# State updates as column tiles and carried state times q as row tiles in batches 1 to 3 of a fused retention and mixer kernel

## The chip, the cores and the metric

One core of a Trainium2 chip runs the whole kernel. The metric is the device time of one execution in microseconds (us). Runs of one kernel scatter by 1 to 2 us to either side here, so every timed comparison below is the kernel against the kernel before, executed in turn on the same chip. A profile is one execution of each kernel; its "span" runs from the first to the last instruction and is about 2 us shorter than the device time. A run more than 1.5% above the fastest of its kernel is called slow, the others fast; ratios use fast runs alone.

## The reference

Two stages in sequence. Retention with one decay per head (4 batches, 8 heads, 768 steps, head size 64), then a mixer with a low-rank product over the sequence and an MLP.

```python
state = gamma * state + einsum('bhd,bhe->bhde', k[:, :, t], v[:, :, t])
y[:, :, t] = scale * einsum('bhd,bhde->bhe', q[:, :, t], state)
...                                     # x: y as (batch, 768, 512)
h = xt @ U @ V                          # rank 32, over the sequence
u = x + h.transpose(0, 2, 1)
out = u + maximum(u @ w_ch1, 0) @ w_ch2 # 512 -> 2048 -> 512
```

The kernel runs the recurrence in chunks of 128 steps. Per chunk: scores (k transposed times q, masked), the output (scores times v, plus carried state times q), and the state update (k transposed times v, summed in PSUM over the chunks). Decays are folded into q and k beforehand.

## The kernel before

Batches 1 to 3 run chunk by chunk between pieces of the MLP of the batch in front of them; a list of start points ("at" and "lag") says where between those pieces each block stands. The parts that the change and the argument touch (cuts marked with `...`):

```python
RINGS = {...}        # PSUM banks by use: "s" has two banks, "o" one, "st" one

def turn_dma(b, ci):                     # batches 2 and 3
    ...
    (nc.sync if b > 2 else nc.scalar).dma_start_transpose(
        out=qkT, in_=qkd.rearrange("p n h d -> p (n h d)"))

def state(b, ci):                        # two heads a matmul, 128x128
    ...
    for p in range(4):
        nc.tensor.matmul(st_p[:, ts(p, P)], qkd[:, 1, ds(2 * p, 2)],
                         vb[:, ds(2 * p, 2)], start=(ci == 0 and p == 0), ...)
    for i in range(2):                   # only the diagonal 64x64 squares
        r = ds(D * i, D)
        evac("A", ns[r, :, r], four(st_p)[r, :, r])

def score(b, ci):
    sp = [bank("s") for _ in range(2)]
    for h in range(H):                   # row tiles: even heads 0-63, odd 64-127
        r = ds(D * (h % 2), D)
        nc.tensor.matmul(sp[h % 2][:, ts(h // 2, P)], qkT[r, 4 + h // 2],
                         qkT[r, h // 2], start=True, stop=True)
    ...                                  # VectorE masks into a[0], a[1]

def mix(b, ci):
    o_p = bank("o")
    if ci:
        for p in range(4):               # carried state times q, whole array
            nc.tensor.matmul(o_p[:, ts(p, P)], qkT[:, p], state[:, p], ...)
    for i in range(2):
        for h in range(i, H, 2):
            nc.tensor.matmul(o_p[:, ts(h, D)], a[i][:, h // 2], vb[:, h], ...)
    evac("A", xs[b][:, ci], o_p)         # one ScalarE copy, 128x512
...
lag = [0.12, 0.17, 0.23] if b == 2 else [0.1, 0.12, 0.2]  # state, score, mix
```

The state sits in SBUF as pairs of heads in 128x128 squares whose off-diagonal halves are zero, so half of each whole-array matmul multiplies zeros or is thrown away.

Of the kernel before, what the change touches and what calls it, by code (L numbers as in the profile page):

```python
# [18 lines left out]
def kernel(  # L19
# [11 lines left out]
    nc = tc.nc  # L31
    P = 128
    B, H, S, D = q.shape
# [11 lines left out]
    NST = 4  # L45
# [26 lines left out]
    def bank(tag, dtype=fp32):  # L72
        n_bank[0] += 1
        ring = RINGS[tag]
        ring.append(ring.pop(0))
        return psum.tile([P, 2048 // (4 if dtype == fp32 else 2)], dtype,
                         tag=f"bank{ring[-1]}", name=f"{tag}_{n_bank[0]}",
                         bufs=1)

    def four(t):  # L80
        return t.rearrange("p (n m) -> p n m", n=4)

    def evac(eng, dst, src):
        if eng == "A":
            nc.scalar.activation(dst, src, AF.Copy)  # L85
        else:
            nc.vector.tensor_copy(out=dst, in_=src)  # L87
# [136 lines left out]
    states = []  # L224
    for i in range(NST):
        t = consts.tile([P, 4, P], bf16, name=f"state{i}")
# [68 lines left out]
    xs = {}  # L295
    live = {}
    n_state = [0]
# [20 lines left out]
    def state_half(sc, x):  # L318

        kd, vb = pre["k", sc], pre["v", sc]  # L320
        first = sc == 0 and x == 0
        if first:
            live["st_p"] = bank("st")
            live["st", 0, 0] = None
        st_p = live["st_p"]
        r = ds(HP * x, HP)
        for par in range(2):
            for p in range(4):
                nc.tensor.matmul(st_p[:, ts(p, P)], kd[r, par, ds(2 * p, 2)],  # L329
                                 vb[r, par, ds(2 * p, 2)],  # L330
                                 start=(first and par == 0 and p == 0),
                                 stop=True, skip_group_check=True)
        ns = states[n_state[0] % NST]
        n_state[0] += 1
        for i in range(2):
            ri = ds(D * i, D)
            evac("A", ns[ri, :, ri], four(st_p)[ri, :, ri])
        live["st", sc + x, 1 - x] = ns

    def score_block(sc, par, tag="s", engs="DD"):  # L340
        kT, qT = live["k", sc], live["q", sc]
        sp = [bank(tag) for _ in range(2)]
        for p in range(4):
            for i in range(2):
                for x in range(2):
                    r = ds(D * i, D)
                    nc.tensor.matmul(sp[i][ds(HP * x, HP), ts(p, P)],
                                     kT[r, p, x, ds(HP * par, HP)],
                                     qT[r, p, x], start=True, stop=True,
                                     skip_group_check=True)  # L350
        for i in range(2):
            a = blk.tile([P, 4, P], bf16, tag=f"a0{i}{par}",
                          name=f"a0{i}{par}_{sc}")
            m = mask0[:, par, None, :].to_broadcast([P, 4, P])
            if engs[i] == "D":
                nc.vector.tensor_tensor(a, four(sp[i]), m, op=ALU.mult)
            else:
                t = blk.tile([P, 4, P], bf16, tag="a_raw", bufs=1,
                              name=f"a_raw_{sc}")
                evac("A", t, four(sp[i]))  # L360
                nc.gpsimd.tensor_tensor(a, t, m, op=ALU.mult)
            live["a", sc, par, i] = a
# [45 lines left out]
    def state(b, ci):  # L408
        qkd, vb = pre.pop((b, ci))
        live[b, ci].append(live.get(("state", b)))  # L410
        if ci < NCK - 1:
            if ci == 0:
                live["st_p", b] = bank("st")
            st_p = live["st_p", b]
            for p in range(4):
                nc.tensor.matmul(st_p[:, ts(p, P)], qkd[:, 1, ds(2 * p, 2)],  # L416
                                 vb[:, ds(2 * p, 2)],
                                 start=(ci == 0 and p == 0), stop=True,
                                 skip_group_check=True)
            ns = states[n_state[0] % NST]  # L420
            n_state[0] += 1
            for i in range(2):
                r = ds(D * i, D)
                evac("A", ns[r, :, r], four(st_p)[r, :, r])
            live["state", b] = ns

    def score(b, ci):
# [12 lines left out]
    def mix(b, ci):  # L440
        if ci == 0:
            xs[b] = xp.tile([P, NCK, DM], fp16, tag="x", name=f"x_{b}")
        vb, qkT, state, *a = live.pop((b, ci))
        o_p = bank("o")
        if ci:
            for p in range(4):
                nc.tensor.matmul(o_p[:, ts(p, P)], qkT[:, p], state[:, p],  # L447
                                 start=(p == 0), stop=False,
                                 skip_group_check=True)
        for i in range(2):  # L450
            for h in range(i, H, 2):
                nc.tensor.matmul(o_p[:, ts(h, D)], a[i][:, h // 2], vb[:, h],  # L452
                                 start=(ci == 0 and h == 0), stop=True,
                                 skip_group_check=True)
        evac("A", xs[b][:, ci], o_p)



# [336 lines left out]
    for b in range(1, B + 1):  # L795
# [9 lines left out]
        if b < B:  # L805
# [11 lines left out]
            else:  # L817
# [4 lines left out]
                if b == 2:  # L822
                    for i, f in enumerate(w2_sums(4) + w2_sums(6)):
                        d = 0.04 + 0.025 * i
                        tracks.append(([f], d, d))
                turn = turn_dma
            for i in range(NCK):
                for f, d in ((turn, 0), (state, lag[0]), (score, lag[1]),
                             (mix, lag[2])):
                    tracks.append(([part(f, b, i)], at[i] + d, at[i] + d))  # L830
            t = at[-1] + lag[2]
# [43 lines left out]
```

## Time and profile before

| | before |
|---|---|
| device time, median of 3 runs | 224.11 us (223.7 to 224.51) |
| span of the profile | 223.0 us |
| TensorE busy | 214.5 us, 96% |
| state blocks, carried blocks | 15 and 15, of four 128x128 matmuls each |
| TensorE instructions on the page, matmuls plus weight loads | 2149 + 2152 = 4301 |

TensorE (PE) is the bound; what matters of it is quoted in the prediction (columns: start, length, engine, source line, operation, result and operands, tile, shape, count). Three more places of the same profile also belong here. The first is PE at the first score block of batch 3 (columns: start, length, engine, source line, operation, result and operands, tile, shape, count):

```profile
139.16 0.39 PE L416 MATMUL st<-vd,qkd 128*128 128x128 bf16 x4
139.38 1.03 PE L640 MATMUL mlp<-uT,w1b 128*128 128x512 f16 x4
140.34 0.40 PE L432 MATMUL s<-qkT 64*128 64x128 bf16 x8
```

The score block starts at 140.34 us without a recorded wait, but its operand, a transpose by DMA, landed at 140.29: there is hardly any slack, 0.05 us. The second is the queue that issues these transposes, SyncE's:

```profile
135.61 1.24 SPq L507 DMA_TRANSPOSE uT<-x  x1
136.90 6.91 SPq L404 DMA_TRANSPOSE qkT<-qkd  x5
```

They are issued back to back, 1.2 to 1.3 us each; the first of q and k is issued at 136.90 and lands 3.39 us later. The third is a line of the page that I passed over before predicting, under the DMA queues (packets, MB, share of 16 engines):

```profile
q8 instruction: 17, 0.28, 0.6%
```

Seventeen transfers of 16 KB on a queue of their own fetch instructions. 4301 instructions on 17 fetches is about 253 each.

### The profile page before, as it was taken

The page shows a single profiled execution, that of the slowest core. Times are in us where ns is not written, and L with a number is a line of the kernel's source. Part 1 is how long each engine was busy: PE and PEld are TensorE (multiplying, and loading weights), DVE is VectorE, ACT ScalarE, POOL GpSimd, SP SyncE. Part 2 cuts the span into 40 slices and gives each one's busy share as a digit, 9 for nine tenths or more (in the row PEclk, how much of TensorE's full clock was granted, in tenths as well). Part 3 has the DMA queues.
Part 4 walks back from the last instruction along what each step waited for, and adds up shares of the span by engine and source line. Part 5 has one row for each costly group of instructions (what it writes and reads, how often), then busy time and mean ns, then how long its engine had stood idle before and what let it go on. Part 6 is the DMA issues. An engine that isn't in the chain of part 4 may idle for free.

```text
span 223.0 us, 5337 instructions
## 1 busy us (share of the span) xinstructions
PE 214.5 (96%) x2149; PEld 144.2 (65%) x2152; DVE 142.2 (64%) x284; ACT 88.0 (39%) x180; POOL 83.5 (37%) x121
## 2 busy tenths in 40 slices
PE   7899899999999998999999999999999999999993
PEld 2466644485555553666688874766887856668882
DVE  6478465333947476599996843786868443867452
ACT  3255645465465315657611005767420035550000
POOL 6442578868867775613757602000000000000000
PEclk9999999999999999999999999999999999999999
DMA  5998799999999999999999999920002734000123
GB/s 163 298 291 205 212 342 299 301 388 239 226 206 212 209 251 209 227 299 167 239 203 222 238 206 215 189 45 11 3 0 85 182 116 47 0 0 4 38 105 142
DMA packets 94633, 39.22 MB, mean 176 GB/s; under 512 B 78096, under 2 KB 87312, under 8 KB 94608
## 3 DMA queue, kind: packets, MB, share of 16 engines
q1 hardware_dynamic: 87408, 35.73, 67.8%
q10 hardware_dynamic: 7200, 3.15, 7.2%
q8 instruction: 17, 0.28, 0.6%
q14 instruction: 8, 0.07, 0.1%
HBM read 27.85 MB, written 6.29 MB: 153 GB/s over the span
## 4 chain that ended last, share of the span: by engine, by line
PE 79%; DVE 8%; SPq 5%; DMA 3%; ACT 1%; issue 1%; ACTq 1%; POOL 0%; DVEq 0%; POOLq 0%
PE mlp L640 32%; PE A L562 14%; PE mlp L685 9%; PE C L562 7%; SPq L142 5%; PE B L562 4%; DMA in<-in_q_dram 3%; PE s L432 2%; DVE gS L515 2%; DVE a L437 2%; PE o L452 2%; PE qk L396 1%; PE o L447 1%; PE st L416 1%; PE s L480 1%
## 5 line engine op out<-in xcount | busy, mean ns | idle before, releaser
L640 PE MATMUL mlp<-uT,w1b 128*128 128x512 f16 (+1 forms) x512 | 89.2, 326 | 0.5 <-DVE uT L87 0.5
L647 ACT ACTIVATE gT<-mlp 128x512 f16<-128x512 f32 (+1 forms) x94 | 45.5, 491 | 63.6 <-PE mlp L640 59.3
L640 PEld LDWEIGHTS <-w1b 128*128 128x128 f16 x512 | 48.1, 98 | 30.8 <-issue 1.2
L645 DVE TENSOR_SCALAR gT<-mlp 128x512 f16<-128x512 f32 (+1 forms) x34 | 18.9, 554 | 27.2 <-PE mlp L640 27.2
L437 DVE TENSOR_TENSOR a<-s,mask 128x512 bf16<-128x512 f32 x36 | 23.1, 682 | 10.7 <-PE s L432 10.7
L562 PEld LDWEIGHTS <-gT 128*128 128x128 f16 x288 | 27.4, 98 | 3.8
L264 POOL TENSOR_TENSOR qkd<-in,gk 128x512 bf16<-128x512 f32 x18 | 19.8, 1100 | 13.1 <-DMA in<-in_k_dram 12.6
L264 POOL TENSOR_TENSOR qkd<-in,gq 128x512 bf16<-128x512 f32 x18 | 19.2, 1066 | 13.9 <-DMA in<-in_q_dram 11.4
L685 PE MATMUL mlp<-w2b,gT 128*128 128x512 f16 x96 | 24.2, 380 | 0.0
L562 PEld LDWEIGHTS <-gS 128*128 128x128 f16 x216 | 21.0, 98 | 2.7
L85 ACT ACTIVATE x<-o 128x512 f16<-128x512 f32 x21 | 12.5, 595 | 21.0 <-PE o L452 19.9
L562 PE MATMUL A<-w2t,gT 128*128 128x256 f16 x144 | 18.4, 273 | 0.0
L85 ACT ACTIVATE state<-st 64x256 bf16<-64x256 f32 x40 | 15.0, 375 | 5.0 <-PE st L329 3.8
L262 POOL CAST vd<-in 128x512 bf16<-128x512 f32 x18 | 11.8, 655 | 6.2 <-DMA in<-in_v_dram 3.4
L685 PEld LDWEIGHTS <-gT 128*128 128x128 f16 x96 | 8.1, 98 | 7.2
L178 PE MATMUL mlp<-ones 128*128 128x512 bf16 x32 | 10.3, 451 | 1.8 <-DVE ones L171 1.4
L484 DVE TENSOR_TENSOR x<-s,x 128x256 f16<-128x256 f32 (+1 forms) x16 | 8.2, 552 | 4.6 <-PE st L480 2.4
L291 POOL CAST w2b<-in 128x512 f16<-128x512 f32 x16 | 9.8, 616 | 3.2 <-DMA in<-in_moe_w_ch_dram 2.6
L285 POOL CAST w1b<-in 128x512 f16<-128x512 f32 x16 | 9.6, 615 | 1.8 <-DMA in<-in_moe_w_ch_dram 1.4
L85 ACT ACTIVATE qkT<-qk 128x1024 bf16<-128x1024 bf16 x6 | 6.1, 1024 | 8.3 <-PE qk L396 8.3
L562 PE MATMUL B<-w2b,gT 128*128 128x256 f16 x72 | 9.3, 273 | 0.0
L562 PE MATMUL C<-w2t,gS 128*128 128x256 f16 x72 | 9.3, 273 | 0.0
(116 smaller groups left out, 261.2 us busy)
## 6 DMA issues: line engine op xcount, KB each, us to landing
in<-in_moe_w_ch_dram SPq DMA_DIRECT2D x32, 256.0 KB, 5.8
in<-in_k_dram SPq DMA_DIRECT2D x24, 256.0 KB, 5.4
in<-in_q_dram SPq DMA_DIRECT2D x24, 256.0 KB, 5.4
in<-in_v_dram SPq DMA_DIRECT2D x24, 256.0 KB, 5.6
out_dram<-o SPq DMA_DIRECT2D x12, 256.0 KB, 2.0
out_dram<-o SPq DMA_DIRECT2D x12, 128.0 KB, 4.3
out_dram<-o ACTq DMA_DIRECT2D x6, 256.0 KB, 4.4
Vf<-in_moe_V_dram SPq DMA_DIRECT2D x4, 96.0 KB, 3.8
```

Source lines behind the costliest of these rows:

```text
L85: nc.scalar.activation(dst, src, AF.Copy)
L142: nc.sync.dma_start(out=t, in_=src)
L178: nc.tensor.matmul(idle_bank[0], ones[:, :P], ones, start=True, stop=True, skip_group_check=True)
L262: nc.gpsimd.tensor_copy(out=t, in_=src)
L264: nc.gpsimd.tensor_tensor(t, src, g[:, ci, :, None].to_broadcast([P, H, D]), op=ALU.mult)
L291: nc.gpsimd.tensor_copy(out=w2b[:, m], in_=take("w2", m))
L437: nc.vector.tensor_tensor(a, four(sp[i]), causal(mask), op=ALU.mult)
L562: nc.tensor.matmul(acc[key, i], lhs[:, m, ts(i, P)], rhs[:, m], start=(fresh and m == 0), stop=(m == NH - 1), skip_group_check=True)
L640: nc.tensor.matmul(g_p[:, :sz], w1b[:, c, ts(m, P)], uTs[b][:, ds(j, nj), c], start=(c == 0), stop=(c == NCB - 1))
L645: nc.vector.tensor_relu(gT[:, m, ds(lo, sz)], g_p[:, :sz])
L647: nc.scalar.activation(gT[:, m, ds(lo, sz)], g_p[:, :sz], AF.Relu)
L685: nc.tensor.matmul(ch, gT[:, m, ts(j, P)], w2b[:, m], start=(m == 0), stop=(m == NM - 1))
```

## The change

Terms: a matmul holds one operand in the array as weights and streams the other through it in columns. A row tile uses half of the array's rows (64*128 in the profile lines), a column tile half of its columns (128*64); 128*128 is the whole array. PSUM is the memory that matmuls write to, in banks.

The intent: compute only the 64x64 squares that are needed. The state update of each head becomes a column tile (two heads side by side in the array), carried state times q becomes row tiles that write two banks, and the state is kept compact, so that one copy of 128x256 replaces two of 64x256. The output then needs two banks, and takes the second from the ring "s" of the scores.

```diff
-            for p in range(4):
-                nc.tensor.matmul(st_p[:, ts(p, P)], qkd[:, 1, ds(2 * p, 2)],
-                                 vb[:, ds(2 * p, 2)],
-                                 start=(ci == 0 and p == 0), stop=True,
+            for h in range(H):
+                nc.tensor.matmul(st_p[ds(D * (h % 2), D), ts(h // 2, D)],
+                                 qkd[:, 1, h], vb[:, h],
+                                 start=(ci == 0 and h < 2), stop=True,
...
-            for i in range(2):
-                r = ds(D * i, D)
-                evac("A", ns[r, :, r], four(st_p)[r, :, r])
+            evac("A", ns, heads(st_p))
...
-        o_p = bank("o")
+        o_p = [bank("s"), bank("o")]
         if ci:
-            for p in range(4):
-                nc.tensor.matmul(o_p[:, ts(p, P)], qkT[:, p], state[:, p],
-                                 start=(p == 0), stop=False,
+            for h in range(H):
+                r = ds(D * (h % 2), D)
+                nc.tensor.matmul(o_p[h % 2][:, ts(h // 2, D)], qkT[r, h // 2],
+                                 state[r, h // 2], start=(h < 2), stop=False,
...
-                nc.tensor.matmul(o_p[:, ts(h, D)], a[i][:, h // 2], vb[:, h],
-                                 start=(ci == 0 and h == 0), stop=True,
+                nc.tensor.matmul(o_p[i][:, ts(h // 2, D)], a[i][:, h // 2],
+                                 vb[:, h], start=(ci == 0 and h < 2), stop=True,
...
-        evac("A", xs[b][:, ci], o_p)
+            evac("A", x[:, i], heads(o_p[i]))
```

More of the change, by code (lines that the diff above doesn't have):

```diff
@@ L81, in four, with heads @@
         return t.rearrange("p (n m) -> p n m", n=4)
+    def heads(t):
+        return t[:, :4 * D].rearrange("p (n d) -> p n d", n=4)
     def evac(eng, dst, src):
@@ L414, in state @@
             st_p = live["st_p", b]
-            for p in range(4):
-                nc.tensor.matmul(st_p[:, ts(p, P)], qkd[:, 1, ds(2 * p, 2)],
-                                 vb[:, ds(2 * p, 2)],
-                                 start=(ci == 0 and p == 0), stop=True,
+            for h in range(H):
+                nc.tensor.matmul(st_p[ds(D * (h % 2), D), ts(h // 2, D)],
+                                 qkd[:, 1, h], vb[:, h],
+                                 start=(ci == 0 and h < 2), stop=True,
                                  skip_group_check=True)
-            ns = states[n_state[0] % NST]
+            ns = states[n_state[0] % NST][:, :2].rearrange(
+                "p n (x d) -> p (n x) d", x=2)
             n_state[0] += 1
-            for i in range(2):
-                r = ds(D * i, D)
-                evac("A", ns[r, :, r], four(st_p)[r, :, r])
+            evac("A", ns, heads(st_p))
             live["state", b] = ns
@@ L443, in mix @@
         vb, qkT, state, *a = live.pop((b, ci))
-        o_p = bank("o")
+        o_p = [bank("s"), bank("o")]
         if ci:
-            for p in range(4):
-                nc.tensor.matmul(o_p[:, ts(p, P)], qkT[:, p], state[:, p],
-                                 start=(p == 0), stop=False,
+            for h in range(H):
+                r = ds(D * (h % 2), D)
+                nc.tensor.matmul(o_p[h % 2][:, ts(h // 2, D)], qkT[r, h // 2],
+                                 state[r, h // 2], start=(h < 2), stop=False,
                                  skip_group_check=True)
+        x = xs[b][:, ci].rearrange("p (n two d) -> p two n d", n=4, two=2)
         for i in range(2):
             for h in range(i, H, 2):
-                nc.tensor.matmul(o_p[:, ts(h, D)], a[i][:, h // 2], vb[:, h],
-                                 start=(ci == 0 and h == 0), stop=True,
+                nc.tensor.matmul(o_p[i][:, ts(h // 2, D)], a[i][:, h // 2],
+                                 vb[:, h], start=(ci == 0 and h < 2), stop=True,
                                  skip_group_check=True)
-        evac("A", xs[b][:, ci], o_p)
+            evac("A", x[:, i], heads(o_p[i]))
     us, uTs, pcs = {}, {}, {}
```

## The prediction

> **What bounds the kernel now.** I read the page first: the busy shares and the chain of work that ended last.
>
> ```profile
> PE 214.5 (96%) x2149; PEld 144.2 (65%) x2152; DVE 142.2 (64%) x284; ACT 88.0 (39%) x180; POOL 83.5 (37%) x121
> ...
> PE 79%; DVE 8%; SPq 5%; DMA 3%; ACT 1%; issue 1%; ACTq 1%; POOL 0%; DVEq 0%; POOLq 0%
> ```
>
> TensorE (PE) is busy 96% of the span and carries 79% of the chain; the granted clock is full in every slice. So the change is judged by the PE time that it adds or removes, except where the chain is on another engine. Second, the groups by shape between 52 and 180 us, where batches 1 to 3 run between the MLP pieces of the batch before.
>
> ```profile
> L416 PE MATMUL st<-vd,qkd 128*128 128x128 bf16 x60 | 5.8, 219 | 0.0
> L447 PE MATMUL o<-state,qkT 128*128 128x128 bf16 x60 | 5.8, 219 | 0.0
> ```
>
> These two groups are all that the change touches on PE: 15 blocks of four for the state update, 15 blocks of four for carried state times q. The 219 ns is latency. What a matmul costs is its slot, start to start, and that comes from the timeline. Here is PE around chunk 1 of batch 3:
>
> ```profile
> 142.86 0.39 PE L416 MATMUL st<-vd,qkd 128*128 128x128 bf16 x4
> 143.09 0.60 PE L640 MATMUL mlp<-uT,w1b 128*128 128x256 f16 x4
> 143.52 0.40 PE L452 MATMUL o<-vd,a 128*128 128x64 bf16 x8
> 143.76 0.60 PE L640 MATMUL mlp<-uT,w1b 128*128 128x256 f16 x4
> 144.29 0.40 PE L432 MATMUL s<-qkT 64*128 64x128 bf16 x8
> 144.62 0.61 PE L640 MATMUL mlp<-uT,w1b 128*128 128x256 f16 x4
> ```
>
> A block of four 128x128 matmuls takes 143.09 - 142.86 = 0.22 us, 56 ns each. Four with 256 columns take 0.43 us (143.09 to 143.52), eight with 64 columns 0.24 us (29 ns each). But the four 256-column ones in front of the score block take 143.76 to 144.29 = 0.53 us: PE loses 0.10 us before a block that uses row tiles (64*128). The score block of eight 64x128 then takes 0.33 us. Run two at a time, its four pairs would need 4 x 56 = 0.22 us, so it loses another 0.11 us on the way back to whole-array matmuls. A tiled block pays about 0.21 us for its two changes of tiling. The low-rank projection, in column tiles 128*32, shows the same:
>
> ```profile
> 166.28 1.04 PE L562 MATMUL A<-w2t,gT 128*128 128x256 f16 x8
> 167.25 0.52 PE L470 MATMUL o<-x,Ub 128*32 128x128 f16 x24
> 167.70 0.50 PE L562 MATMUL B<-w2b,gT 128*128 128x256 f16 x3
> ```
>
> Eight of 256 columns need 0.87 us but take 0.97 (0.10 lost going in). The 24 tiles are six groups of four: 6 x 56 = 0.34 us, and they take 0.45 (0.11 lost going out). And this, from batch 0, is the tempo of row-tile pairs with 64 moving columns into two banks:
>
> ```profile
> 15.59 0.19 PE L380 MATMUL o<-v,a 64*128 64x64 bf16 x1
> 15.59 0.19 PE L380 MATMUL qk<-v,a 64*128 64x64 bf16 x1
> 15.62 0.19 PE L380 MATMUL o<-v,a 64*128 64x64 bf16 x1
> 15.62 0.19 PE L380 MATMUL qk<-v,a 64*128 64x64 bf16 x1
> ```
>
> Two start together, the next pair 0.03 us (29 ns) later: tiles of different row groups do run side by side.
>
> **What the Trainium skill says.** "TensorEngine Tiling (Array Packing)", Key Properties, says that changing the tiling mode drains TensorE. It gives no figure; the trace agrees and puts it at about 0.10 us each way. "TensorE: Matmul & The Clock Gate", Part 3 (The mechanism), says that tiles overlap with starts about 4 ns apart; the trace agrees (pairs start together above). The tiling page's Instruction Overhead warns not to take a tiling factor out of a dimension that is already small; here the tiled matmuls move only 64 columns, so a block has little streaming to save. "PSUM — Partial Sum Buffer", PSUM bank collisions, says that different row tiles may not write one PSUM bank at the same time; hence the second bank of this change. No run here shows that error.
>
> **The change part by part.**
>
> (1) State update: 4 matmuls of 128x128 (0.22 us) become 8 of 128x64 in two column tiles. Four pairs at 29 ns are 0.12 us, saving 0.11; entering and leaving the tiling costs 0.21. First-pair fill is in that 0.21. Net +0.11 us a block (0.33 for 0.22).
>
> (2) Carried state times q: the same sum with row tiles, 0.22 to 0.33 us, net +0.11.
>
> (3) 30 such blocks: the instruction order of the changed kernel shows that nothing moves; 29 are surrounded by whole-array work (MLP, transposes, or the 128-row a-times-v). Only chunk 2 of batch 3 has a state block directly before a carried one, which saves one change of tiling. 30 x 0.108 - 0.11 = +3.1 us of PE work.
>
> (4) ScalarE: state evacuation becomes one copy of 128x256 (about 0.385 us, as the 128x256 relu) for two of 64x256 (0.375 each): 15 x 0.365 = -5.5 us. The x evacuation becomes two of about 0.385 for one of 0.594: 18 x 0.18 = +3.2 us. Net -2.3 us on an engine that is 39% busy: worth next to nothing.
>
> (5) Part of (3) falls into waits that PE has anyway. The best case is in batch 2:
>
> ```profile
> 110.07 0.39 PE L447 MATMUL o<-state,qkT 128*128 128x128 bf16 x4
> 110.37 0.29 PE L452 MATMUL o<-vd,a 128*128 128x64 bf16 x4
> 110.97 0.29 PE L452 MATMUL o<-vd,a 128*128 128x64 bf16 x4 [0.31 <-DVE a L437]
> ```
>
> Here the chain of waits lies on VectorE from 99.26 to 110.92 us (gS, gT and masks back to back), and PE waits 0.08 + 0.49 us for the masks, after 0.07 us at 101.5. In that stretch (from 94.3 us on VectorE runs without a gap) PE gets 4 state and 3 carried blocks, +0.76 us, of which 0.63 us vanish. Then 0.05 us at 115.5, 0.10 us at 53.8 (score waits for qkT) and 0.10 of a 0.24 us wait at 76.6. Absorbed together: 0.88 us. Left of (3): +2.2 us.
>
> (6) A new wait. The output now takes a bank of the ring "s", which has two banks, both used by every score block. The next chunk's score block writes its first half to the other bank and its second half to the one that the mix has just used, so its second matmul waits for ScalarE to read the first half of the output. In the changed kernel's instruction order those matmuls do wait for ScalarE. In batches 1 and 2 there is 0.4 to 1.7 us of other matmuls in between, which is enough. In batch 3 three score blocks (148.4, 153.0, 162.0 us) follow the mix at once:
>
> ```profile
> 161.44 0.39 PE L447 MATMUL o<-state,qkT 128*128 128x128 bf16 x4
> 161.66 0.40 PE L452 MATMUL o<-vd,a 128*128 128x64 bf16 x8
> 161.99 0.40 PE L432 MATMUL s<-qkT 64*128 64x128 bf16 x8
> 162.09 0.60 ACT L85 ACTIVATE x<-o 128x512 f16<-128x512 f32 x1 [3.13 <-PE o L452]
> ```
>
> Worked out for this one, counted from the start of the last matmul of the first half: result after 0.193 us (its latency), ScalarE starts about 0.05 later (here 162.09 - 162.06), reads for 0.385, and PE resumes about 0.055 later (qkT to score in batch 1): 0.68 us. PE without a wait gets there after five slots of 29 ns plus 0.10 for the tiling: 0.24 us. Stall 0.44 us. At 153.0 ScalarE is still on a relu (152.67 to 153.27): 0.48. At 148.4 a relu (to 148.45) and the state copy stand in front: 0.60. At 144.3, with 0.43 us of MLP between: about 0.15. Sum +1.7 us.
>
> Sum: 3.1 - 0.9 + 1.7 = +3.9 us, all of it before batch 3 ends. Batch 4's MLP behind it has PE back to back, so it reaches the end.
>
> **The rivals.** (A) The intent: tiles halve the PE time, 30 x 0.11 = -3.2 us, 220.9 us (1.4% faster). For it: the pairs do run side by side, and two ScalarE copies become one. Against: every tiled block in the trace pays 0.2 us. It would need a change of tiling to be free where weights were loaded ahead; the score blocks, loaded ahead too, say no. (B) Only the tiling costs, and the bank is free in time: 226.3 us. For it: the halves are copied separately, so the first starts early. Against: the three score blocks that follow at once. (C) The column tiles run at 56 ns a pair rather than 29, because 64 weight columns can't be loaded fast enough: another 15 x 3 x 27 ns = 1.2 us, 229.2 us. The trace has no 128*64 tile; in batch 0, 64*64 tiles keep 56 ns with 128 moving columns, which doesn't decide it. (D) The extra copies queue behind relus and stall scores in batch 2 as well, where ScalarE also spends 1.46 us issuing a transpose (94.53): +0.5 to 1 us. Against: those copies stand ahead of the next transpose in the queue.
>
> **Range and chances.** 224.1 + 3.9 = 228.0 us. Low end: no stalls, 226.3, rounded to 226.4. High end: C and part of D with the absorption kept, 229.3. Slower by over 2% begins at 228.6, which needs about 0.6 us more than the sum: 0.24. Faster by over 2% needs -4.5 us, more than A gives: 0.02. Within 2%: 0.74.
>
> **What would show it.** In the changed profile: state and carried blocks of eight at 0.33 us including the 0.10 lost in front (right), or 0.12 (A right); pair spacing 29 ns in 128*64 tiles (else C); in batch 3 at three score blocks a PE wait of 0.4 to 0.6 us released by ScalarE's x copy (else B); the gap at 110.4 us shrunk from 0.57 to near nothing; ScalarE's busy time about 2 us down. I am wrong if tiling changes are cheaper beside column tiles, or if VectorE's chain in batch 2 moves with PE, so that nothing is absorbed (then 228.9).

## The result, and the profile after

| | before | after |
|---|---|---|
| device time, median (range), same rounds | 224.31 us (223.7 to 225.12), 4 runs | 230.23 us (229.37 to 231.0), 4 runs |
| ratio, 95% interval | | 1.026, 1.021 to 1.031: slower |
| span of the profile | 223.0 us | 229.2 us |

Ratios here and below are the mean time of one kernel's fast runs over that of the other's fast runs of the same rounds, so not quite the ratio of the medians that are quoted.

The page of the changed kernel, its busy line and its chain of work that ended last:

```profile
PE 219.3 (96%) x2272; PEld 142.1 (62%) x2272; DVE 143.1 (62%) x284; ACT 84.4 (37%) x183; POOL 83.3 (36%) x121
...
PE 75%; DMA 13%; DVE 4%; POOL 2%; ACT 2%; issue 1%; SPq 1%; DVEq 0%
```

PE's busy time grew by 4.8 us, and the DMA share of the chain rose from 3% to 13%. Most of that is the loading stage, where the chain happens to run through input transfers in this profile, but the page gives 2% to the transposes of q and k, which are not named in the chain of the kernel before: something besides PE's own work took part. PE now has 2272 + 2272 = 4544 instructions on the page, 243 more.

Next, PE before the score block of chunk 2 of batch 3 (chunks count from 0), with both new kinds of block and the score block behind them:

```profile
151.84 0.32 PE L419 MATMUL st<-vd,qkd 128*64 128x64 bf16 x8
152.09 0.20 PE L450 MATMUL s<-state,qkT 64*128 64x64 bf16 x1
152.10 0.20 PE L450 MATMUL o<-state,qkT 64*128 64x64 bf16 x1
152.13 0.19 PE L450 MATMUL s<-state,qkT 64*128 64x64 bf16 x1
152.13 0.19 PE L450 MATMUL o<-state,qkT 64*128 64x64 bf16 x1
...
152.31 0.29 PE L456 MATMUL s<-vd,a 128*128 128x64 bf16 x4
152.44 0.28 PE L456 MATMUL o<-vd,a 128*128 128x64 bf16 x4
152.66 0.23 PE L434 MATMUL s<-qkT 64*128 64x128 bf16 x1
153.15 0.38 PE L434 MATMUL s<-qkT 64*128 64x128 bf16 x7 [0.27 <-ACT x L88]
153.46 2.78 PE L644 MATMUL mlp<-uT,w1b 128*128 128x512 f16 x20
```

The pairs do run side by side, and yet a block is no shorter: the state block takes 151.84 to 152.09 = 0.25 us and the carried one 152.09 to 152.31 = 0.22 us, as long as the whole-array blocks (0.22), and each loses about 0.10 us more in front of it for the change of tiling. Matched block by block with the kernel before, a state block costs 0.13 us more in all and a carried block 0.106.

The last lines show the new wait. The first score matmul starts at 152.66 and the second half only at 153.15: the block takes 153.46 - 152.66 = 0.80 us instead of 0.33, because ScalarE must first read the first half of the output ("ACT x") out of the shared bank. The profile's 0.27 us counts from the end of the matmul in front and so misses a part of it. The table of waits between 140 and 170 us:

```profile
PE s L434 <- DMA qkT<-qkd: 1.2, 1, 1.2
PE s L434 <- ACT x L88: 0.7, 3, 0.3
```

By start times, the four score blocks of batch 3 lose 0.48, 0.45, 0.41 and 0.13 us to the shared bank, 1.5 us together. The first row is one that I had not predicted. Here it is on PE, to be set beside the three lines of the kernel before:

```profile
141.71 0.32 PE L419 MATMUL st<-vd,qkd 128*64 128x64 bf16 x8
141.96 1.04 PE L644 MATMUL mlp<-uT,w1b 128*128 128x512 f16 x4
144.18 0.40 PE L434 MATMUL s<-qkT 64*128 64x128 bf16 x8 [1.18 <-DMA qkT<-qkd]
144.51 1.70 PE L644 MATMUL mlp<-uT,w1b 128*128 128x256 f16 x14
```

PE stands still for 1.2 us in front of the first score block of batch 3. SyncE's queue at that stage:

```profile
138.08 1.24 SPq L511 DMA_TRANSPOSE uT<-x  x1
139.37 7.19 SPq L407 DMA_TRANSPOSE qkT<-qkd  x5
```

The transpose was issued when the rest of the kernel would have it (2.47 us later than before, PE being 2.56 us later here), but landed 4.77 us after its issue and not 3.39. The DMA view says why it may be. First the changed kernel from 141 to 144 us, in 40 slices, with its queues; then the kernel before in the same stage, 138.5 to 141.5 us:

```profile
GB/s 222 205 198 174 222 181 218 222 212 157 355 178 123 113 143 205 164 113 51 27 0 3 10 7 7 10 10 7 10 10 7 10 10 157 276 307 266 48 225 294
...
q1 hardware_dynamic: 1479, 0.37, 123.8%
q8 instruction: 1, 0.02, 1.8%
```

```profile
GB/s 242 236 208 198 218 198 218 201 236 174 198 171 161 92 140 195 212 212 225 205 222 212 205 188 212 208 215 188 181 178 202 110 72 147 205 236 201 242 188 232
```

In the changed kernel the traffic stands nearly still for about 13 slices of 0.075 us, 1 us, with 0 to 10 GB/s. In the same window lies one instruction fetch (q8), which begins at 141.75 us; 141.75 + 0.65 is where the standstill begins. In the kernel before the traffic never drops below 72 GB/s, and no fetch lies in the window: its fetches fall at 134.63 and 147.04 us, on either side of the transposes that somebody waits for. The fetches follow PE's instructions, and the change adds 240 of these. Counted in the traces of all thirteen kernels profiled, 246 to 253 PE instructions lie between two fetches on average (single gaps differ much more), and the twelfth fetch, the one at 147.04 and at 141.75 us, begins after 2968 to 3023 of them, at whatever time that is.

One more surplus of this one profile, 0.8 us at 57 to 58 us (a chunk of batch 1 waits for its input), is absent in other profiles of the same kernel and present in some of other variants: scatter.

### The profile page after: what moved, and what is told of

It reads as the page before. It is cut to its first block, busy times and chain, and to the rows that moved or that the text cites.

```text
span 229.2 us, 5580 instructions
## 1 busy us (share of the span) xinstructions
PE 219.3 (96%) x2272; PEld 142.1 (62%) x2272; DVE 143.1 (62%) x284; ACT 84.4 (37%) x183; POOL 83.3 (36%) x121
## 4 chain that ended last, share of the span: by engine, by line
PE 75%; DMA 13%; DVE 4%; POOL 2%; ACT 2%; issue 1%; SPq 1%; DVEq 0%
PE mlp L644 26%; PE A L566 14%; PE mlp L689 8%; PE C L566 7%; DMA in<-in_moe_w_ch_dram 6%; DMA in<-in_q_dram 5%; PE B L566 3%; PE mlp L181 3%; PE s L434 3%; DMA qkT<-qkd 2%; POOL qkd L267 2%; DVE a L359 2%; PE s L456 1%; PE st L419 1%; PE s L450 1%
## 5 line engine op out<-in xcount | busy, mean ns | idle before, releaser
L651 ACT ACTIVATE gT<-mlp 128x512 f16<-128x512 f32 (+1 forms) x94 | 46.0, 491 | 69.7 <-PE mlp L644 53.0
L267 POOL TENSOR_TENSOR qkd<-in,gk 128x512 bf16<-128x512 f32 x18 | 19.1, 1062 | 19.4 <-DMA in<-in_k_dram 19.0
L88 ACT ACTIVATE x<-s 128x256 f16<-128x256 f32 x18 | 6.9, 382 | 20.5 <-PE s L456 20.4
L181 PE MATMUL mlp<-ones 128*128 128x512 bf16 x34 | 11.4, 468 | 1.4 <-DVE ones L174 1.4
L88 ACT ACTIVATE state<-st 128x256 bf16<-128x256 f32 (+1 forms) x25 | 9.5, 381 | 4.8 <-PE st L332 3.8
L434 PE MATMUL s<-qkT 64*128 64x128 bf16 x144 | 7.9, 218 | 1.9 <-DMA qkT<-qkd 1.2
```

The costliest lines, as they stand in the source:

```text
L88: nc.scalar.activation(dst, src, AF.Copy)
L181: nc.tensor.matmul(idle_bank[0], ones[:, :P], ones, start=True, stop=True, skip_group_check=True)
L267: nc.gpsimd.tensor_tensor(t, src, g[:, ci, :, None].to_broadcast([P, H, D]), op=ALU.mult)
L651: nc.scalar.activation(gT[:, m, ds(lo, sz)], g_p[:, :sz], AF.Relu)
```

## The experiments

To compare profiles without the scatter of the loading stage, I take for each the time from the first transposes of batch 1 (52.12 us in the kernel before) to the end of the span: 223.0 - 52.12 = 170.9 us before. The last column is what each profile has over that. The kernels from after_again to mix_early shared their rounds, so did those from swap_banks to fused, and the last three.

| run | what it is | median us (range), runs | ratio, 95% interval | from batch 1 on, over before |
|---|---|---|---|---|
| first | the changed kernel | 230.23 (229.37 to 231.0), 4 | 1.026, 1.021 to 1.031 | +6.1 |
| after_again | the same once more | 230.32 (229.47 to 231.81), 4 | 1.025, 1.021 to 1.030 | +5.1 |
| state_only | column tiles only | 227.64 (226.56 to 230.05), 4 | 1.011, 1.007 to 1.015 | +5.6 (a slow run) |
| carry_only | row tiles only | 231.29 (229.83 to 232.92), 4 | 1.029, 1.022 to 1.036 | +8.0 |
| mix_early | mix 0.02 earlier in batch 3 | 229.71 (228.75 to 231.38), 4 | 1.024, 1.019 to 1.030 | +3.8 |
| swap_banks | the banks in the other order | 231.99 (231.88 to 232.38), 4 | 1.029, 1.023 to 1.035 | +7.0 |
| after_shift | +54 PE instructions at the start | 229.81 (228.83 to 231.03), 6 | 1.019, 1.014 to 1.023 | +4.7 |
| before_shift | before, +156 | 224.9 (223.96 to 228.57), 22 | 0.997, 0.994 to 0.999 | +0.2 |
| fused | before, row tiles beside the scores | 224.82 (223.63 to 227.53), 22 | 0.998, 0.996 to 1.001 | -0.9 |
| after_shift2 | +96 PE instructions at the start | 228.56 (228.24 to 229.21), 6 | 1.018, 1.014 to 1.022 | +4.0 |
| before_shift2 | before, +198 | 225.49 (224.59 to 227.34), 21 | 1.005, 1.003 to 1.007 | +0.6 |
| after_both | after_shift2 with mix_early | 226.85 (226.63 to 227.74), 6 | 1.010, 1.006 to 1.014 | +2.4 |

The kernel before had a median of 224.97, 225.61 and 224.72 us in the three groups of rounds (7, 43 and 26 runs). All kernels gave correct results.

My theory after the first profile, called F in the last expectations (the rival of scatter is J there): the surplus over the predicted sum is an instruction fetch that the longer instruction stream pulled into the transposes of batch 3. The rivals: scatter of the DMA, and the changed blocks themselves costing more than counted.

### The same kernel again

No edit.

> The changed kernel once more. The changed kernel's first profile was 6.2 us longer than that of before. Counted block by block on the matmul engine, 4.0 us of it are what the change does (tiled blocks and waits for the shared bank); 0.8 us is a wait for the first inputs of batch 1 (chunk 1's q and k landed about 0.9 us later than in the profile of before) and 1.3 us a wait for the first transposed q and k of batch 3, which took 4.8 us from issue to landing and not 3.4. Theory Luck: both are DMA jitter, so here at least one of them is gone or clearly smaller and the time over before falls towards +4.0 us (228.3). Theory Systematic: both come again at the same places with about the same size, and the time stays at +5.5 to +6.2 us.

The time came out the same. The wait at 57 us was gone, so that one is scatter. The wait of the first score block of batch 3 was there again: 1.13 us over the kernel before, with a landing of 4.61 us and a fetch at 140.32 us, 1.8 us after that transpose was issued. That one is not scatter.

### Each half alone

Column tiles alone, with the state in the wide layout and everything behind it as before:

```diff
-            evac("A", ns, heads(st_p))
+            for i in range(2):
+                r = ds(D * i, D)
+                evac("A", ns[r, :, r], heads(st_p)[r])
...             # mix: one bank, whole-array matmuls, one copy, as before
```

> Only the state update as column tiles; its result is spread to the old block-diagonal state by two copies, carried state times q and its output are as before. From the changed kernel's profile a state block costs 0.13 us more than before (0.35 for 0.22), 15 of them 1.95 us; 0.1 us vanishes in the wait for qkT at the first block and about 0.5 us in batch 2 where VectorE sets the pace. Expected +1.3 us (225.6). If tiling changes were cheap beside column tiles, it would be at or under 224.3. No wait of a score block for an x copy may appear.

State blocks cost 0.13 us more each, as in the changed kernel. The time rose by 1.1%, about 2.5 us, against an expected 1.3: a miss. In its profile (which fell on the slowest of its runs, so I take positions from it and not the total) batch 2 does not swallow its share: PE's waits for the masks of chunk 3 are 1.05 us there and 0.55 in the kernel before. And it has a new wait, in 120 to 150 us:

```profile
PE mlp L643 <- DMA uT<-x: 1.3, 1, 1.3
```

The fetch lies at 131.55 us here, among the two transposes of the mixer's u (uT<-x) that the next MLP starts with, which took 4.87 and 5.42 us instead of 3.35 and 3.19. A kernel with 120 more PE instructions has its fetches elsewhere, and they hit another transpose. I had not foreseen that: taking half of the change away does not take half of this cost away. Whether the fast runs have this wait too, no profile shows.

Row tiles alone:

```diff
-            for h in range(H):
-                nc.tensor.matmul(st_p[ds(D * (h % 2), D), ts(h // 2, D)],
-                                 qkd[:, 1, h], vb[:, h], ...)
+            for p in range(4):
+                nc.tensor.matmul(st_p[:, ts(p, P)], qkd[:, 1, ds(2 * p, 2)],
+                                 vb[:, ds(2 * p, 2)], ...)
...
-            evac("A", ns, heads(st_p))
+            for i in range(2):
+                r = ds(D * i, D)
+                evac("A", ns[r], four(st_p)[r, :, r])
```

> Only the carried state times q as row tiles into two banks, with the state update as whole-array matmuls and two copies that write the compact state. 15 blocks at 0.106 us more are 1.6 us, of which about 0.4 us vanish in waits; the waits of score blocks for the x copy stay (1.46 us in the changed kernel, a little more here since two state copies stand before one of them). Expected +2.8 us (227.1). If the shared bank costs nothing on the path, +1.2 us.

A miss: 2.9% and not 1.2%. The profile, of the slowest of the four runs, has the parts that I had expected, but the waits at the score blocks are larger: 0.2 to 1.0 us at five blocks, 2.6 us together where I had expected a little over 1.5. It has others too: 0.9 us at the transposes of u (again with a fetch, at 131.88 us, among them), 0.5 us at the first of q and k of batch 3, and 1.9 us near 97 us, where ScalarE issued a transpose late. At the wait of 0.5 us no fetch of PE's lies, but a transfer of 8 KB on the other instruction queue (q14) does, at 143.65 us, and the transpose took 3.94 us to land. The wait near 97 us is seen in no other profile; the chain leads back from it to an input of q that landed 5 us after its issue, and why it was late stays open. The two halves don't sum to the whole, because what a fetch costs depends on where it happens to fall.

### The mix earlier

```diff
-                lag = [0.12, 0.17, 0.23] if b == 2 else [0.1, 0.12, 0.2]
+                lag = [0.12, 0.17, 0.23] if b == 2 else [0.1, 0.12, 0.18]
```

This puts MLP matmuls between the mix and the next score block.

> The changed kernel with the mixes of batch 3 issued 0.02 of the track earlier, so that every mix has at least 0.86 us of other matmuls behind it before the next score block uses its bank. If the waits for the x copy are what the bank costs, the three stalls of 0.4 to 0.5 us and the one of 0.13 us go and the kernel is 1.4 us faster than the changed kernel of the same call. If they are only where a later wait shows (masks, transposed inputs), the time stays within 0.4 us of it.

The waits between 140 and 170 us, and one of the score blocks that had taken 0.80 us:

```profile
PE s L434 <- DMA qkT<-qkd: 1.1, 1, 1.1
```

```profile
151.72 0.40 PE L434 MATMUL s<-qkT 64*128 64x128 bf16 x8
152.05 2.78 PE L644 MATMUL mlp<-uT,w1b 128*128 128x512 f16 x20
```

The waits for ScalarE's copy are gone and a score block takes 0.33 us again. From the first score block of batch 3 to the end this profile is 1.44 us shorter than the changed kernel's second one, which is the size of the waits. The times alone don't show it (229.71 against 230.32 us, ranges overlapping); the later run with both repairs does. The wait for the transpose stays.

### The banks in the other order

```diff
-        o_p = [bank("s"), bank("o")]
+        o_p = [bank("o"), bank("s")]
```

Now the half in the shared bank is written second, and so read second.

> The changed kernel with the two output banks exchanged: the even heads go to the bank of their own and the odd heads, which are finished and copied last, to the bank shared with the scores. If the score blocks wait for the copy of the shared bank, each of the three waits of 0.41 to 0.48 us in batch 3 grows by the 0.12 us of four matmuls and by the part of the second copy that cannot overlap, 0.28 us: 0.7 to 0.9 us each, and the block at 148 us by the same: about +1.6 us over the changed kernel. If they wait for something else, nothing changes.

```profile
PE s L434 <- ACT x L88: 1.7, 4, 0.5
PE s L434 <- DMA qkT<-qkd: 1.0, 1, 1.0
```

The waits for the copy grew from 0.7 to 1.7 us by the profile's count; each of the four waiting blocks became 0.28 us later, a fifth that had not waited now loses 0.24, and from the first score block of batch 3 on the profile is 1.35 us longer than the changed kernel's (expected 1.6). The time, taken in other rounds, doesn't tell the two apart (ratios 1.029 and 1.025). That the order of two names sets the size confirms what the wait is for.

### Moving the fetch without touching the work

Idle matmuls that the kernel runs in its loading stage are cut into pieces: the same columns, more instructions. If fetches follow the instruction count, this moves them in batch 3 and nothing else there.

```diff
-            nc.tensor.matmul(idle_bank[0], ones[:, :P], ones, ...)
+        for _ in range(n * cut):
+            w = 512 // cut
+            nc.tensor.matmul(idle_bank[0][:, :w], ones[:, :P], ones[:, :w], ...)
...
-        keep_busy(3 if sc else 9, fresh=True)
+        keep_busy(3 if sc else 9, fresh=True, cut=1 if sc else 4)
```

In the changed kernel, 54 more instructions:

> The changed kernel with its first nine idle matmuls of 512 columns cut into 36 of 128: 54 more TensorE instructions at the very start, the same streaming time. In all profiles so far a 16 KB fetch of TensorE instructions goes over the DMA engines about every 256 instructions, at fixed places in the program; in three profiles of the changed order it fell into the transposes of batch 3's first chunks (139 to 142 us), which then took 4.6 to 4.8 us to land, and the first score block waited 1.1 to 1.3 us. In the kernel before no fetch falls there. Theory Fetch: 54 instructions more bring that fetch to about 136 us, ahead of the transposes; they land in 3.4 us again, the first score block of batch 3 does not wait (under 0.1 us over the state block's own cost), and the kernel is about 1.1 us faster than the changed kernel, near +4.3 us over before. Theory Luck: the landing stays long in about every case, wherever the fetch is.

The fetch moved to 138.65 us, from 141.75 in the changed kernel's first profile and 140.32 in its second: 1.7 to 3.1 us for 54 instructions (4544 instructions in 229 us are 20 a microsecond, so 2.7 us were to be expected). It did not clear the transposes: it now stretched the issue of the one in front (2.04 us on SyncE's queue instead of 1.24), and the score block's wait halved, to 0.63 us. Half a confirmation; the time, 1.9% or about 4.2 us over the kernel before, has too wide an interval to add to it.

In the kernel before, 156 more:

> The kernel before, with idle matmuls at the start cut finer: 156 more TensorE instructions, the same streaming time, nothing else. That should bring the fetch of 147.0 us to about 138.5 us, into the transposes of batch 3's first chunks. Theory Fetch: they take about 4.7 us instead of 3.4 to land, the first score block of batch 3 waits about 1.2 us, and the kernel is about 1.1 us slower than before (225.8 for 224.7) though no work of the change is in it. Theory Luck or a cause inside the change: no wait there, the same time within 0.3 us.

A miss of aim. The fetch came at 141.47 us, later than meant, and stretched the third and fourth transposes to 4.58 and 4.09 us (3.23 and 3.32 before). Nobody waits for these, and the time did not rise (if anything it fell, by 0.3%, and nothing says why). So a fetch stretches transposes in the kernel before too, but it must hit the right one to cost time.

With the rate known, I aimed again. In the changed kernel 96 more instructions (the second set of idle matmuls is cut as well):

```diff
-        keep_busy(0 if sc else 7)
+        keep_busy(0 if sc else 7, cut=1 if sc else 4)
```

> The changed kernel with 96 more TensorE instructions in its first stage (16 short idle matmuls of 512 columns cut in four, the same columns), which should pull the instruction fetch that lies at 141.75 us (140.32 in the second look, 138.65 with 54 instructions more) to about 136 us, between the transposes of the carried chunk and the first one of batch 3. Theory F (the fetch stretches the batch-3 transposes): no transpose of batch 3 from 138 us on takes over 3.5 us from issue to landing, the first score block of batch 3 waits at most 0.1 us longer than in the kernel before (instead of 1.1 to 1.3), and the time falls by about 1.1 us against the changed kernel, to 229.1. Rival J (jitter, or the changed order of the mix itself delays that transpose): the wait of about 1.1 us stays.

The fetch lies at 135.50 us. PE at the first score block of batch 3:

```profile
140.19 0.32 PE L420 MATMUL st<-vd,qkd 128*64 128x64 bf16 x8
140.44 1.04 PE L645 MATMUL mlp<-uT,w1b 128*128 128x512 f16 x4
141.41 0.40 PE L435 MATMUL s<-qkT 64*128 64x128 bf16 x8
```

The wait is gone, the transposes of batch 3 take 3.30 to 3.41 us, and the kernel is at 228.56 us. The same program with 96 instructions more, in a stage 100 us earlier, is 1.1 us shorter from batch 1 on than the changed kernel's second profile (4.0 against 5.1 over the kernel before). The ratio fell from 1.025 to 1.018, in different rounds, and the intervals (1.021 to 1.030, 1.014 to 1.022) just touch; it is the wait in the profiles that shows the cause.

And in the kernel before, 198 more instructions, to bring about what the change had brought about:

```diff
+        keep_busy(3 if sc else 9, fresh=True, cut=1 if sc else 8)
...
+        keep_busy(0 if sc else 7, cut=1 if sc else 4)
...
+            keep_busy(4, cut=4)
...
+            keep_busy(3, cut=1 if sc else 2)
```

> The kernel before with 198 more TensorE instructions in its first stage (idle matmuls cut, the same columns), which should pull the fetch that lies at 147.0 us (141.47 with 156 instructions more) to about 139 us, inside the first two transposes of q and k of batch 3. Theory F: the transpose issued at about 136.9 us takes 4.4 to 4.8 us instead of 3.4, the first score block of batch 3 waits about 1.1 us longer, and the time is about 1.1 us more than that of the kernel before. Rival J: that transpose takes 3.3 to 3.4 us and the time doesn't move. If the fetch misses that stretch again, the run decides nothing on the time.

The fetch lies at 138.81 us, and:

```profile
139.54 0.39 PE L417 MATMUL st<-vd,qkd 128*128 128x128 bf16 x4
139.77 1.03 PE L641 MATMUL mlp<-uT,w1b 128*128 128x512 f16 x4
141.80 0.40 PE L433 MATMUL s<-qkT 64*128 64x128 bf16 x8 [1.01 <-DMA qkT<-qkd]
```

The traffic from 138 to 141 us, in 40 slices, has the same standstill:

```profile
GB/s 198 208 205 184 195 147 86 99 178 208 406 222 198 218 164 133 79 34 24 3 0 0 3 7 7 10 7 10 10 10 7 14 7 10 102 273 294 290 290 294
```

The same wait at the same block, in a kernel that has nothing of the change. The transpose took 4.47 us, the block came 1.07 us later, and the time rose by 0.5%, 1.1 us, with an interval (1.003 to 1.007) that lies above 1. Since before_shift moved by 0.3% the other way, a shift of the instructions can have other effects of that size, and the time alone would be thin evidence. (The profile's total shows only +0.6 because batch 2 happened to run 0.5 us shorter in it.) With the fetch brought in and taken out at will, theory F stands.

### Both repairs

> The changed kernel with the 96 more TensorE instructions and with the earlier mix in batch 3 (lag 0.18 for 0.20). If the surplus over the kernel before is the sum of tiling (2.2 to 2.5 us after what is absorbed), score waits (1.4) and the stretched transpose (1.1), this kernel keeps the first part alone: about 2.3 us over the kernel before, ratio about 1.010; no wait for the x copy above 0.15 us in batch 3 and none above 0.15 us for the first transpose of q and k. If it stays above 1.018, something else costs the time.

The changed kernel with its fetch moved and its mix earlier is 1.0% slower than the kernel before, as expected, and its profile has no wait of PE between 140 and 170 us. What is left is the tiling. The interval (1.006 to 1.014) lies below that of after_shift2 (1.014 to 1.022), so the waits for the copy are worth time as well: 0.8%, about 1.8 us (1.6 between the two profiles).

### A version where the tiling pays

If a row-tiled block costs 0.21 us for two changes of tiling, it should stand where the array is in row tiles anyway: directly behind a score block. This version starts from the kernel before, keeps whole-array state updates, and in batches 1 and 3 runs carried state times q right behind the scores of its chunk, into a bank of its own ("x").

```diff
+        if b in FUSED and ci:            # at the end of score(b, ci)
+            o_p = live["o_p", b, ci] = two_banks(b, ci)
+            for h in range(H):
+                r = ds(D * (h % 2), D)
+                nc.tensor.matmul(o_p[h % 2][:, ts(h // 2, D)], qkT[r, h // 2],
+                                 state[r, h // 2], start=(h < 2), stop=False,
...
-                lag = [0.12, 0.17, 0.23] if b == 2 else [0.1, 0.12, 0.2]
+                lag = [0.12, 0.17, 0.23] if b == 2 else [0.1, 0.12, 0.18]
```

> An attempt to beat both, from the kernel before: the state update stays whole-array and is copied into a compact state (batches 1 and 3); carried state times q in row tiles runs right behind the score block of the same chunk, which is in the same tiling already, into two banks that are not the scores' (MLP gives one up); the mixes of batch 3 are issued 0.02 earlier. If only the change of tiling made the row tiles dear, a carried block now costs 4 pairs of 29 ns, 0.12 us for 0.22, and 10 of them save 1.1 us of TensorE time over before (223.6). Rival: the bank that MLP loses, or the output copies in front of the next block, make waits that give it back (224.7 or more).

```profile
143.74 0.40 PE L442 MATMUL s<-qkT 64*128 64x128 bf16 x8
143.97 0.19 PE L448 MATMUL x<-slim,qkT 64*128 64x64 bf16 x1
143.98 0.19 PE L448 MATMUL o<-slim,qkT 64*128 64x64 bf16 x1
144.00 0.19 PE L448 MATMUL x<-slim,qkT 64*128 64x64 bf16 x1
144.00 0.19 PE L448 MATMUL o<-slim,qkT 64*128 64x64 bf16 x1
...
144.19 1.04 PE L667 MATMUL mlp<-uT,w1b 128*128 128x256 f16 x6
```

The scores take 143.74 to 143.97 = 0.23 us here, and the carried block 143.97 to 144.19, of which the way back to the whole array, which the scores would otherwise have paid, is about half: the carried block adds 0.11 to 0.12 us instead of 0.33. Its profile is 0.9 us shorter than the kernel before from batch 1 on; the time (ratio 0.998, interval 0.996 to 1.001) does not tell it from the kernel before, so it leaves the expectation undecided, while the changed kernel's interval (1.021 to 1.031) is far above. No version clearly beat the kernel before.

## Why the prediction was wrong

Predicted were 228.0 us and 226.4 to 229.3; the kernel took 230.2. The mechanisms listed were right and their sizes nearly so; the sum lacked a term.

- **Step 1 (state block, +0.11 us).** Measured +0.13. The pairs start 0.053, 0.031 and 0.032 us after one another, so the tempo is 31 ns, but the second pair comes 0.02 us late (in the carried block the pairs are 0.038, 0.029 and 0.029 us apart). A term off by a fifth: 15 x 0.02 = 0.3 us. (The prediction's rounded figures, 0.21 lost and 0.11 saved, give 0.10; it used 0.108.)
- **Step 2 (carried block, +0.11 us).** Measured +0.106. Right.
- **Step 3 (30 blocks, +3.1 us).** 15 x 0.13 + 15 x 0.106 - 0.11 (chunk 2 of batch 3, where the two stand together) = +3.4 us. Right but for the term above.
- **Step 4 (ScalarE -2.3 us, worth nothing).** State copies went from 40 x 375 ns to 15 x 384 and 10 x 375 ns, 5.4 us less; the output copies from 12.5 to 15.6 us, 3.1 more: net -2.3 us, as worked out (its busy time fell by 3.6 us in all). That nothing came of it is right too.
- **Step 5 (0.88 us absorbed).** The ten state and ten carried blocks of batches 1 and 2 cost 10 x 0.13 + 10 x 0.106 = 2.36 us; from the first transposes of batch 1 to the projection of batch 2 the changed kernel's second profile is 1.49 us longer. So 0.87 us vanished, about half of it at the gap near 110 us, where PE's waits fell from 0.55 to 0.12 us. The mechanism is right; that the sum agrees to the hundredth is luck, since this stretch differs by 0.7 to 0.9 us between profiles whose work in it is the same.
- **Step 6 (new wait, +1.7 us).** The four predicted score blocks waited, 0.48, 0.45, 0.41 and 0.13 us, together 1.5 us against 0.60, 0.48, 0.44 and 0.15 predicted. Right; taking the wait away (mix_early, after_both) and doubling it (swap_banks) confirm the cause.
- **The sum, +3.9 us, "all of it before batch 3 ends".** This is the step that failed. 3.4 - 0.9 + 1.5 = +4.0 us is what its own terms measured, and after_shift2, the changed kernel without the fetch in the way, shows just that: +4.0 us from batch 1 on, 228.56 us, inside the range. The changed kernel itself has 1.1 to 1.3 us more, because its 240 additional PE instructions move a 16 KB instruction fetch into the transposes of batch 3, on the one that PE had no slack for. The prediction took every operand to be there in time: it asked what the new instructions cost to run, not what it costs to fetch them. Nor did it look at the slack of operands by DMA: 0.05 us at the block at 140.34 us.
- **The rest.** The first profile has 0.8 us more that is scatter of the input. 5.1 us of the second profile against 5.3 us between the medians of its rounds leaves nothing else of size.

Of the rivals, A (tiles halve the time) fell: no block got shorter, except in the fused version, where the condition that A named, a change of tiling that is not paid, holds. B fell with the waits of step 6. C fell: the pairs run at 31 ns and not at 56. D did not occur: no score block of batch 2 waits for a copy. In "What would show it", the points came out on the side of the sum (with 0.35 us for a state block in place of 0.33); none of them looked at the transposes.

What stays open: how a fetch holds up the transposes. The trace shows that traffic stands still for about 1 us from some 0.6 to 1.1 us after the fetch begins, in every profile where one fell among several transposes in flight on SyncE's queue, and that moving the fetch moves this; it does not show what the two share. Open too are the late issue near 97 us in the run with row tiles alone, and the part that scatter has in the first result.

## What to carry to other kernels

Before packing small matmuls into tiles, count the changes of tiling: here one costs about as much as four pairs of 64 columns save, so tiles pay only beside work that is already in that tiling. Before giving an output a bank of another ring, look at who takes that bank next, and how soon. And where an engine's instruction count changes, look at what its instruction fetches will fall on: an operand by DMA that lands just in time is a cost waiting for a shift elsewhere in the program.

## What the Trainium skill lacked or had wrong

- "Runtime: NRT & Kernel Launch", Instruction fetch mechanics: that fetches come in 16 KiB blocks of 256 instructions agrees (246 to 253 PE instructions between two fetches of 16 KB on average). That the cost of crossing a block is "mostly hidden" lacks the effect on others: DMA transposes on SyncE's queue that had one among them took 3.5 to 5.4 us instead of 3.2 to 3.4, and where the first one was waited for the kernel lost 1.1 us.
- "DMA: Bandwidth & Descriptors", DMA Transpose (X-bar): nothing on this contention either, nor a duration for a transpose from SBUF of this size; here one of q and k for a chunk takes 1.2 to 1.3 us to issue and 3.0 to 3.4 us to land on SyncE's queue in batch 3, but 4.9 to 6.7 us on ScalarE's in batch 2, in the profile of the kernel before.
- "TensorEngine Tiling (Array Packing)", Key Properties: the drain on a change of tiling mode has no figure. Here it is about 0.10 us on each side of a block, between whole-array and row tiles as between whole-array and column tiles; from column tiles directly to row tiles it is 0.10 us too (0.13 us start to start, where 0.03 is a slot).
- The same page, Instruction Overhead: right in direction, but without a break-even. Here eight tiled matmuls of 64 columns take 0.22 to 0.25 us with one change of tiling, where four whole-array ones of 128 columns take 0.22 us; behind other row tiles the eight take 0.12 us.
- "TensorE: Matmul & The Clock Gate", Part 3: starts of tiles about 4 ns apart agree within a pair (3 to 4 ns). Between pairs of 64 columns the runs show 29 ns in row tiles, and 31 ns in column tiles with the second pair 0.02 us late; the page has no such numbers.
